# A linear-attention block with an MLP on one Trainium2 core: two transposes go from TensorE to DMA, and the order of the start and of the second layer norm changes

## The chip, the cores and the metric

The kernel runs on one core of a Trainium2 chip. The metric is the device time of one execution in microseconds (us), lower is better. The engines run side by side, each through its own list of instructions in order, and wait for each other by semaphores: PE (TensorE, matrix products), DVE (VectorE), ACT (ScalarE), POOL (GpSimd) and SP (SyncE). Here SP issues all DMA transfers.

## The reference, cut to what matters

Input x has 2048 rows of 512; there are 32 heads of 16; the MLP is 1792 wide. All is bf16.

```
def _layernorm(x, axis=-1, eps=1e-5):
    m = jnp.mean(x, axis=axis, keepdims=True)
    v = jnp.var(x, axis=axis, keepdims=True)
    return (x - m) / jnp.sqrt(v + eps)
phi = lambda t: jnp.where(t > 0, t + 1, jnp.exp(t)) + 1e-6
...
pq, pk = phi(q), phi(k)
kv = jnp.einsum("bhsd,bhse->bhde", pk, v)
z = jnp.einsum("bhsd->bhd", pk)
num = jnp.einsum("bhqd,bhde->bhqe", pq, kv)
den = jnp.einsum("bhqd,bhd->bhq", pq, z)[..., None] + 1e-6
o = num / den
...
h = x + _A_ref(_layernorm(x, axis=-1), A_wqkv, A_wo)
h2 = h + _B_ref(_layernorm(h, axis=-1), B_w1, B_w2)
```

_B_ref is max(y @ w1, 0) @ w2.

## The kernel before

The 2048 rows are 16 tiles of 128 (t), in 4 chunks of 512 (c, tiles 4c to 4c+3). The order of all work is written out by hand: the string ORDER is a list of words, each a small function with its numbers, and every engine gets its instructions in the order of the words. A word's name is the function op_ with that name. A number that names a PSUM bank (there are eight of 512 float32) is not needed below. The words that matter:

- Start, per tile: lx loads x (SP); S and A are the statistics (bn_stats, bn_aggr; DVE, L248, L249); R is 1/std (two ACT instructions, L254, L255); N normalises (DVE, L262); T transposes the tile by four PE transposes (L287) and E copies them from PSUM (ACT, L297); from tile 5 on X transposes by one DMA instead (SP, L308). The result lnT has the features on the partitions.
- K (per tile, 4 matmuls of 512 columns, L316) and Q (per chunk and block of 128 features, 4 matmuls, L324) are the projections of keys and queries. F, U, M, D and qF, qU, qM, qD make phi of them (two on ACT, two on DVE). lk and lq load their weights, wk_sb and wq_sb.
- G, z, kv, m: the sums over all rows, folded with wv and wo into m_sb.
- Per chunk: d4 the denominators (PE), dl4 and dx4 their reciprocals (ACT), wb stores these to DRAM (SP, L468), eight rb load them back, spread over the partitions (SP, L471), and dm multiplies the queries by them (two DVE instructions, L484, result pqs).
- Per tile, the second layer norm: h (4 matmuls from pqs, L493), hD adds x (DVE, L499), s and a the statistics (L250, L251), n subtracts the mean (DVE, L270; nA does the same on ACT, L276), and x transposes by DMA (L309), or t by PE with v copying on DVE (L306). r is 1/std (ACT), applied only at the end.
- Per chunk and block f of 128 of the MLP's 1792: p (4 matmuls of 512 columns, L508; ph does it in two halves of 256 columns, tiles 0, 1 and tiles 2, 3, L517), and pD (DVE, L528) or pA (ACT, L523) evicts two blocks with the relu. Then per tile f (14 matmuls, L537), fo (DVE, L545: times 1/std plus h) and fd (the store, SP, L552; four buffers).

PE, DVE and SP take their words strictly in turn, so a word that waits holds all later words of its engine. What keeps a word from its engine is its inputs, its PSUM bank, and its buffer. All rb of all chunks write one buffer, rr. A transposing DMA of one tile is one instruction on SP, an rb eighth is one too.

In the first chunk before the change, tiles 0 and 1 of the second layer norm are normalised on ACT (nA) and transposed by DMA, tiles 2 and 3 are normalised on DVE and transposed by PE. Only the blocks f = 0 to 3 are done in halves.

Of the kernel before, what the change touches and what calls it, by code (L numbers as in the profile page):

```python
# [15 lines left out]


ORDER = """
table const masks warm.70.7.64 warm.2.7 lx.0.1 S.0 A.0 R.0.1 lx.1.1 S.1 lx.2.1 A.1 N.0 T.0.1 lk.0.4 S.2 R.1.1
N.1 T.1.2 lx.3.1 A.2 E.0 K.0.4 R.2.1 lx.4.2 S.3 N.2 T.2.1 E.1 A.3 S.5 R.3.1 K.1.0.0.2 K.1.0.2.2 N.3 S.4 A.5 A.4  # L20
E.2 T.3.2 K.2.6.0.2 K.2.6.2.2 F.0.1 M.0.1 lx.6.2 E.3 S.7 lq.0.4 R.4.2 lx.8.4 Q.0.3.1 N.4 U.0.1 A.7 F.1.1 F.2.1
T.4.2 N.5 S.6 Q.0.1.4 U.1.1 M.1.1 A.6 lx.12.4 M.2.1 D.0.1 R.6.2 K.3.7.0.2 K.3.7.2.2 E.4 X.5 U.2.1 U.3.1 D.1.1
N.6 Q.0.0.3 N.7 S.10 qF.0.0.2 K.4.5 K.5.6 S.8 A.10 S.9 A.8 qU.0.0.2 S.12 F.4.2 D.2.1 X.6 Q.0.2.0 A.9 A.12 K.6.2
S.13 S.11 M.4.2 A.11 A.13 U.4.2 D.4.2 F.3.1 R.8.2 N.9 M.3.1 X.7 K.7.3 R.12.2 R.10.2 N.8 F.6.2 D.3.1 N.13 S.15
G.0 G.1 U.6.2 S.14 X.9 X.8 N.10 A.14 A.15 N.12 qM.0.0.2 M.6.2 X.13 qF.0.2.2 R.14.2 qU.0.2.2 qM.0.2.2 N.11 G.2
G.3 G.5 G.4 N.14 X.12 K.9.3 K.8.2 K.13.1 N.15 qD.0.0.2 D.6.2 za.4.1 X.11 X.10 F.8.2 U.8.2 M.8.2 K.12.0 U.12.2
F.12.2 G.7 za.6.0 K.11.3 D.8.2 qD.0.2.2 M.12.2 za.8.0 K.10.2 F.10.2 X.14 G.8 K.14.0 U.10.2 X.15 K.15.1 M.10.2 zf
lv.2.2 lv.0.2 G.9 D.10.2 zhi D.12.2 F.14.2 G.6 G.10 G.11 M.14.2 zlo U.14.2 D.14.2 z.0.0 z.2.0 z.3.0 z.1.0 G.14
lo.0.2 lo.2.2 zc zh d4.0.1 dl4.0 l1.0.2 G.13 G.12 G.15 dx4.0 gA.2.2 Q.1.1.3 Q.1.0.2 qF.1.0.2 gD.0.2 kv.1.4
kv.3.4 kv.0.4 kv.2.4 kx qU.1.0.2 qM.1.0.2 qD.1.0.2 Q.1.3.1 Q.1.2.0 qF.1.2.2 m.0.2 m.1.3 mD.0.2 m.3.7 m.2.6 wb.0  # L30
Q.2.0.4 Q.2.1.5 rb.0.7 rb.0.1 rb.0.6 rb.0.3 rb.0.0 rb.0.2 rb.0.4 rb.0.5 l1.2.2 qM.1.2.2 qU.1.2.2 Q.2.3.1
qD.1.2.2 mA.2.2 qF.2.0.2 Q.2.2.0 qU.2.0.2 dm.0.2.2 dm.0.0.2 qM.2.0.2 h.1.6 hD.1 s.1 a.1 qU.2.2.2 d4.1.3 dl4.1
h.0.7 hD.0 s.0 dx4.1 h.2.6 h.3.5 a.0 l2.0.7 wb.1 hD.2 nA.1 hD.3 qF.2.2.2 nA.0 s.2 s.3 Q.3.0.2 Q.3.1.3 a.2
Q.3.3.6 a.3 qF.3.0.2 qU.3.0.2 Q.3.2.5 x.1 r.0.4 qF.3.2.2 n.2 t.2.7 n.3 t.3.4 qD.2.0.2 v.2 v.3 x.0 ph.0.3.1.0
ph.0.1.3.0 ph.0.2.0.0 ph.0.3.1.1 qM.2.2.2 qM.3.0.2 ph.0.0.2.0 ph.0.0.2.1 qM.3.2.2 qD.3.0.2 qU.3.2.2 qD.2.2.2
ph.0.2.0.1 qD.3.2.2 p.0.7.5 d4.2.6.2 pD.0.2.2 dl4.2 dl4.3 rb.1.4 rb.1.6 rb.1.3 rb.1.2 rb.1.0 rb.1.1 ph.0.1.3.1
rb.1.7 rb.1.5 p.0.6.4 dx4.2 dm.1.0.2 dm.1.2.2 h.4.0 pD.0.0.2 hD.4 pD.0.6.2 p.0.5.1 h.6.6 dx4.3 p.0.4.0 hD.6
l2.7.7 h.5.4 pA.0.4.2 s.4 s.6 hD.5 h.7.7 a.4 a.6 p.0.11.6 p.0.10.5 s.5 hD.7 a.5 p.0.9.4 wb.2 rb.2.6 n.4 rb.2.0
rb.2.4 s.7 n.6 rb.2.3 rb.2.2 rb.2.1 a.7 n.5 n.7 rb.2.5 rb.2.7 dm.2.0.2 dm.2.2.2 pD.0.10.2 p.0.13.1 p.0.12.0
p.0.8.3 pD.0.12.2 wb.3 r.4.4 rb.3.0 rb.3.4 h.10.7 hD.10 x.6 h.8.2 h.11.6 hD.8 s.10 rb.3.5 rb.3.1 rb.3.6  # L40
f.1.0.0.7 rb.3.3 rb.3.2 rb.3.7 s.8 hD.11 pD.0.8.2 h.9.5 f.3.1.0.7 x.7 x.5 s.11 a.8 hD.9 f.1.0.7.7 f.0.4.0.7 a.10
a.11 x.4 dm.3.2.2 dm.3.0.2 h.14.7 h.12.3 s.9 n.11 h.15.6 a.9 n.10 h.13.2 fo.1 n.9 n.8 hD.14 s.14 hD.12 x.11
hD.15 f.0.4.7.7 r.8.4 p.1.13.7 p.1.6.3 a.14 hD.13 s.12 s.15 s.13 a.12 a.15 a.13 n.14 p.1.12.6 n.13 f.3.1.7.7
n.12 n.15 p.1.2.5 fo.0 pD.1.12.2 x.10 p.1.7.4 fo.3 p.1.3.6 x.9 pD.1.6.2 pD.1.2.2 r.12.4 x.8 p.1.11.2 p.1.10.1
pD.1.10.2 f.2.4.0.7 p.2.0.6 p.2.1.7 f.2.4.7.7 pD.2.0.2 p.2.10.0 p.2.11.1 fo.2 x.14 p.2.6.2 p.2.7.3 x.15 fd.3
p.2.13.7 p.2.12.6 pD.2.10.2 pD.2.6.2 x.12 fd.1 pD.2.12.2 p.2.2.0 x.13 fd.0 p.2.3.1 p.1.5.6 p.1.4.5 pD.2.2.2
pD.1.4.2 p.1.0.3 p.1.1.4 p.1.9.1 p.1.8.0 pD.1.0.2 pD.1.8.2 f.4.4.0.7 f.4.4.7.7 fo.4 fd.4 f.5.3.0.7 f.5.3.7.7
fo.5 fd.2 f.6.7.0.7 f.6.7.7.7 fo.6 p.2.4.2 p.2.5.3 f.7.0.0.7 f.7.0.7.7 pD.2.4.2 fo.7 p.3.6.1 p.3.7.2 pD.3.6.2
p.3.8.3 p.3.9.4 p.3.5.1 pD.3.8.2 p.3.4.0 pD.3.4.2 fd.6 p.3.10.3 p.3.11.4 pD.3.10.2 p.3.2.0 p.3.3.1 p.3.0.5
p.3.1.6 pD.3.2.2 pD.3.0.2 p.3.13.3 fd.7 p.3.12.2 pD.3.12.2 f.10.1.0.7 f.15.2.0.14.3.1 f.15.7.0.14.0.2 p.2.8.4  # L50
p.2.9.5 fo.15.3.1 fd.15.3.1 fo.15.0.2 pD.2.8.2 f.8.7.0.7 f.10.1.7.7 fo.10 f.8.7.7.7 fo.8 f.14.2.0.7 f.14.2.7.7
f.13.3.0.7 fd.5 fd.8 fd.10 fo.14 f.13.3.7.7 fo.13 f.9.0.0.7 f.9.0.7.7 fd.15.0.2 f.11.6.0.7 f.11.6.7.7 fd.13 fo.9
f.12.0.0.7 fd.9 f.12.0.7.7 fo.11 fd.14 fd.11 fo.12 fd.12 f.15.2.0.14.2.1 fo.15.2.1 fd.15.2.1
"""


# [1 line left out]
def kernel(  # L58
# [166 lines left out]
    def op_tw(n):
        rows = A_wqkv.rearrange("(r s) n -> r s n", s=A_wqkv.shape[0] // n)
        nc.scalar.dma_start(out=first_w[0:n, 0, :], in_=rows[:, 0, D : D + 4])

    def op_tx(n):
        rows = xf.rearrange("(r s) d -> r s d", s=S // n)  # L230
        nc.scalar.dma_start(out=first_x[0:n, :], in_=rows[:, 0, 0:4])

    def op_ta():
        nc.scalar.dma_start(out=first_w[:], in_=wqkv_v[:, :, D : D + 4])
# [234 lines left out]

    def op_rb(c, h):  # L470
        nc.sync.dma_start(  # L471
            out=rr[h * DH : (h + 1) * DH, :, :],
            in_=scr[c][:, h, :, :].rearrange("j o n -> o j n").broadcast_to([DH, KD, CW]),
        )
# [6 lines left out]

    def op_dm(c, jb, n):
        i = (c * KD + jb) % NQ
        nc.vector.tensor_tensor(  # L484
            out=pqs[:, i : i + n, :], in0=pqT[c][:, jb : jb + n, :], in1=rr[:, jb : jb + n, :], op=ALU.mult
        )


# [99 lines left out]
```

## Time and profile before

| | us |
|---|---|
| median of 3 runs | 169.63 (169.54 to 170.61) |
| the profiled execution, its own time | 169.66 |
| its span, first to last instruction | 168.0 |
| PE busy | 162.7 (97%) |
| DVE busy | 115.6 (69%) |
| ACT busy | 49.5 (29%) |
| granted TensorE clock | 1.00 |

The profile is one execution. "PE" is the matmuls, "PEld" the loads of their stationary operands, which overlap matmuls. A group's line gives the source line, the engine, result and input by the program's names, the count, the busy time and what ended the idle time before. In the chain of waits, each piece is the time in which the work that ended last moved on, by line. In the list of waits a line reads: who waited, for whom, total us, times, longest. In the timeline a row is the start, the length, the engine and line, and in brackets how long the engine was idle before, and for what. SPq is SP's queue of DMA issues; its times are those of issuing, and a transfer lands later.

### The profile page before, as it was taken

The numbers are of one execution on the slowest core, as the hardware profiler recorded it, in microseconds if no ns is written. First come the engines' busy times: TensorE is split into PE (matmuls) and PEld (weight loads), VectorE is DVE, ScalarE is ACT, GpSimd is POOL, SyncE is SP. The second block draws the span as 40 slices with busy tenths as digits, with TensorE's granted clock in tenths as the row PEclk, the third lists the DMA queues.
The fourth block names the chain that finished last, engine by engine and source line by source line (L and its number), as shares of the span: only waits on it lengthen the run. The fifth ranks groups of instructions, "written<-read, shape, count | busy, mean of one in ns | idle before, by whom it ended". The sixth has DMA issues, their size and how long they took to land.

```text
span 168.0 us, 2417 instructions
## 1 busy us (share of the span) xinstructions
PE 162.7 (97%) x924; PEld 79.2 (47%) x924; DVE 115.6 (69%) x217; ACT 49.5 (29%) x83; POOL 4.8 (3%) x21
## 2 busy tenths in 40 slices
...
GB/s 108 353 298 88 20 106 95 189 301 45 132 337 161 98 205 132 132 48 123 83 102 57 126 63 0 0 0 0 62 31 35 0 0 7 32 34 48 31 94 39
DMA packets 25003, 16.01 MB, mean 95 GB/s; under 512 B 15008, under 2 KB 23968, under 8 KB 24992
## 3 DMA queue, kind: packets, MB, share of 16 engines
...
q8 instruction: 7, 0.11, 0.3%
q14 instruction: 4, 0.03, 0.1%
HBM read 9.96 MB, written 2.62 MB: 75 GB/s over the span
## 4 chain that ended last, share of the span: by engine, by line
PE 92%; DMA 4%; SPq 2%; DVE 1%; issue 0%
PE bk L537 28%; PE bk L508 27%; PE bk L324 8%; PE bk L368 8%; PE bk L493 8%; PE bk L316 7%; DMA wq_sb<-in_A_wqkv_dram 4%; PE bk L517 2%; SPq L214 2%; PE bk L440 1%; DVE gT L545 1%; PE bk L392 1%; PE bk L414 1%; PE bk L426 1%; PE bk L287 0%
## 5 line engine op out<-in xcount | busy, mean ns | idle before, releaser
L537 PE MATMUL bk<-w_sb,at 128*128 128x512 bf16 (+2 forms) x252 | 50.0, 355 | 0.0
L508 PE MATMUL bk<-lnT,w_sb 128*128 128x512 bf16 x208 | 46.9, 379 | 0.0
L528 DVE TENSOR_SCALAR at<-bk 128x1024 bf16<-128x1024 f32 x27 | 32.8, 1223 | 13.2 <-PE bk L508 13.2
L537 PEld LDWEIGHTS <-at 128*128 128x128 bf16 x252 | 23.5, 98 | 25.4
L508 PEld LDWEIGHTS <-w_sb 128*128 128x128 bf16 x208 | 20.4, 98 | 23.9
L545 DVE SCALAR_TENSOR_TENSOR gT<-bk,rstd,h_nat 128x512 bf16<-128x512 f32 (+2 forms) x18 | 12.4, 691 | 24.6 <-PE bk L537 22.0
L334 ACT ACTIVATE eb<-bk 128x1024 bf16<-128x1024 f32 (+1 forms) x18 | 16.6, 929 | 5.3 <-PE bk L316 2.8
L337 ACT ACTIVATE rb<-bk 128x1024 bf16<-128x1024 f32 (+1 forms) x18 | 16.4, 929 | 0.0
L324 PE MATMUL bk<-lnT,wq_sb 128*128 128x512 bf16 x64 | 15.1, 379 | 0.3 <-DMA wq_sb<-in_A_wqkv_dram 0.3
L316 PE MATMUL bk<-wk_sb,lnT 128*128 128x512 bf16 x64 | 15.3, 379 | 0.0
L493 PE MATMUL bk<-m_sb,pqs 128*128 128x512 bf16 x64 | 15.1, 379 | 0.0
L368 PE MATMUL bk<-at,h_nat 128*128 128x512 bf16 x56 | 13.1, 379 | 0.0
L248 DVE BATCH_NORM_STATS2 st<-x_nat 128x6 f32<-128x512 bf16 x16 | 10.6, 678 | 2.3 <-DMA x_nat<-in_A_x_dram 2.3
L499 DVE TENSOR_TENSOR h_nat<-bk,x_nat 128x512 bf16<-128x512 f32 x16 | 10.6, 676 | 0.9 <-PE bk L493 0.9
L254 ACT ACTIVATE rstd<-mv,eps 128x2 f32<-128x2 f32 (+2 forms) x14 | 4.2, 297 | 23.7 <-DVE mv L251 20.9
L250 DVE BATCH_NORM_STATS2 st<-h_nat 128x6 f32<-128x512 bf16 x16 | 10.5, 684 | 0.1
L324 PEld LDWEIGHTS <-wq_sb 128*128 128x128 bf16 x64 | 6.1, 98 | 7.7 <-DMA wq_sb<-in_A_wqkv_dram 0.8
L493 PEld LDWEIGHTS <-pqs 128*128 128x128 bf16 x64 | 6.1, 98 | 7.7 <-DVE pqs L484 0.6
L368 PEld LDWEIGHTS <-h_nat 128*128 128x128 bf16 x64 | 6.1, 98 | 7.3 <-issue 0.2
L316 PEld LDWEIGHTS <-lnT 128*128 128x128 bf16 x64 | 6.1, 98 | 6.8
L341 DVE TENSOR_SCALAR eb<-eb 128x1024 bf16<-128x1024 bf16 (+1 forms) x18 | 6.6, 389 | 0.0
L262 DVE TENSOR_SCALAR h_nat<-x_nat,mv,rstd 128x512 bf16<-128x512 bf16 x16 | 6.3, 408 | 0.2 <-ACT rstd L255 0.2
...
## 6 DMA issues: line engine op xcount, KB each, us to landing
...
```

The lines of the kernel that those rows point to most:

```text
L248: op_S = lambda t: nc.vector.bn_stats(out=st[:, t, :], in_=x_nat[:, t, :])
L316: nc.tensor.matmul(bk[:, b, :], lhsT=lnT[c][:, kd, j * P : (j + 1) * P], rhs=wk_sb[:, kd, :], start=(kd == 0), stop=(kd == KD - 1),)
L324: nc.tensor.matmul(bk[:, b, :], lhsT=wq_sb[:, kd, j * P : (j + 1) * P], rhs=lnT[c][:, kd, :], start=(kd == 0), stop=(kd == KD - 1),)
L334: nc.scalar.activation(out=buf(eb, kind, i, n), in_=bank(at_bank[kind, i], n), func=ACT.Exp)
L337: nc.scalar.activation(out=buf(rb, kind, i, n), in_=bank(at_bank[kind, i], n), func=ACT.Relu)
L368: nc.tensor.matmul(bk[:, KD + kd, :], lhsT=ln_nat[:, t, kd * P : (kd + 1) * P], rhs=pk(t)[:, 0, :], start=(not stated), stop=(len(stated) ...
L493: nc.tensor.matmul(bk[:, b, :], lhsT=pqs[:, (c * KD + jb) % NQ, j * P : (j + 1) * P], rhs=m_sb[:, jb, :], start=(jb == 0), stop=(jb == KD ...
L499: nc.vector.tensor_tensor(out=h_nat[:, t : t + n, :], in0=bank(at_bank["h", t], n), in1=x_nat[:, t : t + n, :], op=ALU.add,)
L508: nc.tensor.matmul(bk[:, b, :], lhsT=w1_sb[:, kd, f * P : (f + 1) * P], rhs=lnT[c][:, kd, :], start=(kd == 0), stop=(kd == KD - 1),)
L528: nc.vector.tensor_scalar(out=acts[c % 2][:, f : f + n, :], in0=bank(at_bank["p", c, f], n), scalar1=-1.0, scalar2=0.0, op0=ALU.mult, op1= ...
L537: nc.tensor.matmul(bk[:, b, 0 : w * P], lhsT=acts[c % 2][:, f, j * P : (j + 1) * P], rhs=w2_sb[:, f, k * P : (k + w) * P], start=(f == 0), ...
L545: nc.vector.scalar_tensor_tensor(out=o_t[:, t % NO, cols], in0=bk[:, at_bank["f", t, k], 0 : w * P], scalar=rstd2[:, t : t + 1], in1=h_nat ...
```

## The change

- Start: A.2 stands ahead of N.1 on DVE, N.2 ahead of S.3. K.3 (two words of two matmuls each) and Q.0.0 stand ahead of Q.0.3. The order of SP's loads of x and of the first weights stays.
- First chunk's second layer norm: nA.0, nA.1 become n.0, n.1 (on DVE); t.2, t.3, v.2, v.3 become x.2, x.3. The order of tiles is 1, 0, 3, 2 throughout; h.1 stands ahead of Q.2.3.
- On SP, x.1 and x.0 stand ahead of the store wb.1, then x.3, x.2, and then the eight rb.1.
- MLP of the first chunk: the blocks f = 6, 7 are done in halves as well, all six first halves stand ahead of the second halves; pA.0.4 (ACT) becomes pD.0.4 (DVE).
- rr becomes two buffers, one for even and one for odd chunks.
- The remaining words are the same, with other places and other banks. Three functions that no word uses are removed, with two small tiles of theirs, so lines from 223 on have smaller numbers afterwards: 12 less from the layer norms on.

The diff, with the order cut to the two places (before, then after):

```diff
-table const masks warm.70.7.64 warm.2.7 lx.0.1 S.0 A.0 R.0.1 lx.1.1 S.1 lx.2.1 A.1 N.0 T.0.1 lk.0.4 S.2 R.1.1
-N.1 T.1.2 lx.3.1 A.2 E.0 K.0.4 R.2.1 lx.4.2 S.3 N.2 T.2.1 E.1 A.3 S.5 R.3.1 K.1.0.0.2 K.1.0.2.2 N.3 S.4 A.5 A.4
-E.2 T.3.2 K.2.6.0.2 K.2.6.2.2 F.0.1 M.0.1 lx.6.2 E.3 S.7 lq.0.4 R.4.2 lx.8.4 Q.0.3.1 N.4 U.0.1 A.7 F.1.1 F.2.1
+table const masks warm.70.7.64 warm.2.7 lx.0.1 S.0 A.0 R.0.1 lx.1.1 S.1 lx.2.1 A.1 N.0 T.0.1 lk.0.4 S.2 A.2
+R.1.1 N.1 T.1.2 E.0 R.2.1 lx.3.1 N.2 K.0.4 lx.4.2 S.3 T.2.1 E.1 A.3 S.5 R.3.1 K.1.0.0.2 K.1.0.2.2 N.3 S.4 A.5
+A.4 E.2 T.3.2 K.2.6.0.2 K.2.6.2.2 F.0.1 M.0.1 lx.6.2 E.3 S.7 lq.0.4 R.4.2 lx.8.4 K.3.7.0.2 K.3.7.2.2 Q.0.0.3
...
-qD.1.2.2 mA.2.2 qF.2.0.2 Q.2.2.0 qU.2.0.2 dm.0.2.2 dm.0.0.2 qM.2.0.2 h.1.6 hD.1 s.1 a.1 qU.2.2.2 d4.1.3 dl4.1
-h.0.7 hD.0 s.0 dx4.1 h.2.6 h.3.5 a.0 l2.0.7 wb.1 hD.2 nA.1 hD.3 qF.2.2.2 nA.0 s.2 s.3 Q.3.0.2 Q.3.1.3 a.2
-Q.3.3.6 a.3 qF.3.0.2 qU.3.0.2 Q.3.2.5 x.1 r.0.4 qF.3.2.2 n.2 t.2.7 n.3 t.3.4 qD.2.0.2 v.2 v.3 x.0 ph.0.3.1.0
-ph.0.1.3.0 ph.0.2.0.0 ph.0.3.1.1 qM.2.2.2 qM.3.0.2 ph.0.0.2.0 ph.0.0.2.1 qM.3.2.2 qD.3.0.2 qU.3.2.2 qD.2.2.2
-ph.0.2.0.1 qD.3.2.2 p.0.7.5 d4.2.6.2 pD.0.2.2 dl4.2 dl4.3 rb.1.4 rb.1.6 rb.1.3 rb.1.2 rb.1.0 rb.1.1 ph.0.1.3.1
-rb.1.7 rb.1.5 p.0.6.4 dx4.2 dm.1.0.2 dm.1.2.2 h.4.0 pD.0.0.2 hD.4 pD.0.6.2 p.0.5.1 h.6.6 dx4.3 p.0.4.0 hD.6
+Q.2.2.1 rb.0.1 qF.2.0.2 dm.0.0.2 dm.0.2.2 h.1.6 qD.1.2.2 h.0.3 hD.1 s.1 d4.1.4 hD.0 l1.2.2 a.1 dl4.1 n.1 s.0
+dx4.1 h.3.5 a.0 n.0 l2.0.7 x.1 x.0 wb.1 hD.3 Q.2.3.2 s.3 qF.2.2.2 qU.2.2.2 a.3 h.2.3 hD.2 n.3 s.2 Q.3.2.4
+Q.3.3.5 a.2 n.2 Q.3.1.7 Q.3.0.6 x.3 x.2 qF.3.2.2 ph.0.2.0.0 qM.2.2.2 qM.2.0.2 r.0.4 qD.2.2.2 qM.3.2.2 qD.2.0.2
+qU.3.2.2 qF.3.0.2 ph.0.1.3.0 ph.0.0.2.0 rb.1.1 ph.0.3.1.0 ph.0.6.4.0 ph.0.7.5.0 qM.3.0.2 qD.3.2.2 rb.1.5 rb.1.6
+ph.0.2.0.1 ph.0.3.1.1 ph.0.6.4.1 ph.0.7.5.1 qU.3.0.2 qD.3.0.2 pD.0.2.2 d4.2.6.2 pD.0.6.2 ph.0.1.3.1 rb.1.3
+rb.1.7 rb.1.2 ph.0.0.2.1 pD.0.0.2 rb.1.4 dl4.2 rb.1.0 p.0.11.1 dl4.3 dm.1.0.2 dm.1.2.2 l2.7.7 dx4.2 p.0.5.5
+p.0.4.4 h.5.2 wb.2 pD.0.4.2 hD.5 h.4.6 hD.4 h.7.5 s.5 h.6.2 hD.7 a.5 rb.2.4 rb.2.1 hD.6 f.0.3.0.7 s.7 s.4 s.6
...
-    rr = big.tile([P, KD, CW], BF16, name="rr")
+    rr = [big.tile([P, KD, CW], BF16, name=f"rr{i}") for i in range(2)]
...
-            out=rr[h * DH : (h + 1) * DH, :, :],
+            out=rr[c % 2][h * DH : (h + 1) * DH, :, :],
...
-            out=pqs[:, i : i + n, :], in0=pqT[c][:, jb : jb + n, :], in1=rr[:, jb : jb + n, :], op=ALU.mult
+            out=pqs[:, i : i + n, :], in0=pqT[c][:, jb : jb + n, :], in1=rr[c % 2][:, jb : jb + n, :], op=ALU.mult
```

More of the change, by code (lines that the diff above doesn't have):

```diff
@@ L18 @@
 ORDER = """
-table const masks warm.70.7.64 warm.2.7 lx.0.1 S.0 A.0 R.0.1 lx.1.1 S.1 lx.2.1 A.1 N.0 T.0.1 lk.0.4 S.2 R.1.1
-N.1 T.1.2 lx.3.1 A.2 E.0 K.0.4 R.2.1 lx.4.2 S.3 N.2 T.2.1 E.1 A.3 S.5 R.3.1 K.1.0.0.2 K.1.0.2.2 N.3 S.4 A.5 A.4
-E.2 T.3.2 K.2.6.0.2 K.2.6.2.2 F.0.1 M.0.1 lx.6.2 E.3 S.7 lq.0.4 R.4.2 lx.8.4 Q.0.3.1 N.4 U.0.1 A.7 F.1.1 F.2.1
-T.4.2 N.5 S.6 Q.0.1.4 U.1.1 M.1.1 A.6 lx.12.4 M.2.1 D.0.1 R.6.2 K.3.7.0.2 K.3.7.2.2 E.4 X.5 U.2.1 U.3.1 D.1.1
-N.6 Q.0.0.3 N.7 S.10 qF.0.0.2 K.4.5 K.5.6 S.8 A.10 S.9 A.8 qU.0.0.2 S.12 F.4.2 D.2.1 X.6 Q.0.2.0 A.9 A.12 K.6.2
@@ L24 @@
[L24 to L28, printed above, removed]
@@ L29 @@
-lo.0.2 lo.2.2 zc zh d4.0.1 dl4.0 l1.0.2 G.13 G.12 G.15 dx4.0 gA.2.2 Q.1.1.3 Q.1.0.2 qF.1.0.2 gD.0.2 kv.1.4
-kv.3.4 kv.0.4 kv.2.4 kx qU.1.0.2 qM.1.0.2 qD.1.0.2 Q.1.3.1 Q.1.2.0 qF.1.2.2 m.0.2 m.1.3 mD.0.2 m.3.7 m.2.6 wb.0
-Q.2.0.4 Q.2.1.5 rb.0.7 rb.0.1 rb.0.6 rb.0.3 rb.0.0 rb.0.2 rb.0.4 rb.0.5 l1.2.2 qM.1.2.2 qU.1.2.2 Q.2.3.1
-qD.1.2.2 mA.2.2 qF.2.0.2 Q.2.2.0 qU.2.0.2 dm.0.2.2 dm.0.0.2 qM.2.0.2 h.1.6 hD.1 s.1 a.1 qU.2.2.2 d4.1.3 dl4.1
-h.0.7 hD.0 s.0 dx4.1 h.2.6 h.3.5 a.0 l2.0.7 wb.1 hD.2 nA.1 hD.3 qF.2.2.2 nA.0 s.2 s.3 Q.3.0.2 Q.3.1.3 a.2
@@ L34 @@
-Q.3.3.6 a.3 qF.3.0.2 qU.3.0.2 Q.3.2.5 x.1 r.0.4 qF.3.2.2 n.2 t.2.7 n.3 t.3.4 qD.2.0.2 v.2 v.3 x.0 ph.0.3.1.0
-ph.0.1.3.0 ph.0.2.0.0 ph.0.3.1.1 qM.2.2.2 qM.3.0.2 ph.0.0.2.0 ph.0.0.2.1 qM.3.2.2 qD.3.0.2 qU.3.2.2 qD.2.2.2
-ph.0.2.0.1 qD.3.2.2 p.0.7.5 d4.2.6.2 pD.0.2.2 dl4.2 dl4.3 rb.1.4 rb.1.6 rb.1.3 rb.1.2 rb.1.0 rb.1.1 ph.0.1.3.1
-rb.1.7 rb.1.5 p.0.6.4 dx4.2 dm.1.0.2 dm.1.2.2 h.4.0 pD.0.0.2 hD.4 pD.0.6.2 p.0.5.1 h.6.6 dx4.3 p.0.4.0 hD.6
-l2.7.7 h.5.4 pA.0.4.2 s.4 s.6 hD.5 h.7.7 a.4 a.6 p.0.11.6 p.0.10.5 s.5 hD.7 a.5 p.0.9.4 wb.2 rb.2.6 n.4 rb.2.0
@@ L39 @@
[L39 to L53, printed above, removed]
+table const masks warm.70.7.64 warm.2.7 lx.0.1 S.0 A.0 R.0.1 lx.1.1 S.1 lx.2.1 A.1 N.0 T.0.1 lk.0.4 S.2 A.2
```

38 lines of the change are left out of this document (27 added, 11 removed).

## The prediction

> **What bounds the kernel now.** I read the page's busy times first, then the stretches, the start of the timeline, the chain around the removed work, and last what SP's queue does there. Columns of the stretches: start:end, length, then busy us (and instructions) of PE, PEld, DVE, ACT, POOL, granted clock, DMA share, GB/s.
>
> ```profile
> PE 162.7 (97%) x924; PEld 79.2 (47%) x924; DVE 115.6 (69%) x217; ACT 49.5 (29%) x83; POOL 4.8 (3%) x21
> ```
> ```profile
> 5.00:10.40 5.40, 4.13 (x30) 1.85 (x30) 4.87 (x15) 4.43 (x14) 1.05 (x4) 1.00 1.07 380
> 10.40:35.80 25.40, 25.40 (x126) 11.72 (x127) 24.47 (x60) 20.74 (x34) 0.00 (x0) 1.00 0.51 126
> ...
> 60.00:75.00 15.00, 15.00 (x79) 6.71 (x78) 14.80 (x27) 3.83 (x7) 0.00 (x0) 1.00 0.42 129
> 75.00:101.00 26.00, 26.00 (x122) 11.77 (x121) 22.64 (x44) 1.00 (x4) 0.00 (x0) 1.00 0.42 92
> ```
>
> PE has no idle time from 10.4 us to its last matmul near 164.2; it idles only before 10.4. So the time changes in three ways only: less matmul work, less idle time before 10.4, or new holes after it. DVE is nearly full twice (24.47 of 25.40, 14.80 of 15.00), so it is where a hole would come from. The clock is 1.00 in every row, so all PE rows below hold in every stretch.
>
> ```profile
> 5.55 0.47 DVE L262 TENSOR_SCALAR h_nat<-x_nat,mv,rstd 128x512 bf16<-128x512 bf16 x1
> 5.95 0.16 DVE L249 BATCH_NORM_AGGREGATE mv<-st 128x2 f32<-128x6 f32 x1
> 6.08 0.23 PEld L287 LDWEIGHTS <-h_nat 128*128 128x128 bf16 x4 [0.77 <-DVE h_nat L262]
> ...
> 6.62 0.69 DVE L248 BATCH_NORM_STATS2 st<-x_nat 128x6 f32<-128x512 bf16 x1 [0.51 <-DMA x_nat<-in_A_x_dram]
> 7.23 0.40 DVE L262 TENSOR_SCALAR h_nat<-x_nat,mv,rstd 128x512 bf16<-128x512 bf16 x1
> ...
> 9.22 0.60 ACT L297 ACTIVATE lnT<-bk 128x512 bf16<-128x512 bf16 x1
> ...
> 10.38 1.04 PE L324 MATMUL bk<-lnT,wq_sb 128*128 128x512 bf16 x4 [0.33 <-DMA wq_sb<-in_A_wqkv_dram]
> ```
> DVE's order at the start is N.1, A.2, S.3, N.2; S.3 waited for tile 3 until 6.62 and N.2 stood behind it. At the end of the start-up PE waits for wq_sb (landed at 10.33) while K.3's input (E.3, 9.22 to 9.82) lies ready.
>
> ```profile
> 53.25 3.45 PE bk L324 x16
> 56.70 0.45 PE bk L287 x8
> 57.15 3.06 PE bk L517 x28
> ```
> ```profile
> 54.20 1.20 SPq L309 DMA_TRANSPOSE lnT<-hn  x1
> 55.58 3.73 SPq L471 DMA_DIRECT2D rr<-scr  x8
> ```
> ```profile
> PEld L493 <- DVE pqs L484: 0.6, 2, 0.3
> ```
> The chain holds t.2 and t.3 (eight PE transposes, 0.45 us). On SP the eight loads rb.1 follow the transposes x.1, x.0. The weight loads of h wait for DVE's multiply dm.1 by these loads; PE itself doesn't lose by it yet, since weights are loaded ahead.
>
> **The change, part by part.** PE's spacing comes from the chain: a 512-wide matmul 216 ns (0.86 us for 4), 256-wide 109 ns (3.06 for 28), a transpose 56 ns (0.45 for 8).
>
> 1. Start. A.2 now stands ahead of N.1, and N.2 ahead of S.3. S.2 ends at 5.64 (4.95 and 0.69), A.2 runs at 5.68, N.1 at 5.78 in place of 5.55, T.1 at 6.25 in place of 6.08. ACT is in E.0 until about 6.02, then runs R.2 (0.29, 0.20) to 6.55; N.2 starts at 6.59 in place of 7.23. S.3 follows 0.32 behind N.2's start, at 6.91 in place of 6.62; A.3 at 7.64 (7.54 before), and R.3, N.3, T.3, E.3 all about 0.09 later: E.3 ends at 9.9, K.2 runs 9.11 to 9.97. K.3 now comes ahead of the first Q: 4 x 216 ns, 9.97 to 10.83. The first Q then starts at 10.83 with wq_sb half a microsecond in place. Before it started at 10.38 with K.3 (0.86) still to do. Gain 10.38 + 0.86 - 10.83 = 0.41. SP's loads keep their order, so wq_sb's landing stays. Bounds: 0.50 (the whole hole from K.2's last issue to Q), and 0.0, if the pieces ahead slip by another 0.4; nearer the former, as every step has its row. With PE 0.41 earlier, K.7 comes at 17.1 and X.7's transpose (issued at 14.44, landed 2.45 later) is in at 16.9: cover 0.1 to 0.2.
>
> 2. t.2, t.3 go: 8 x 56 ns = -0.45. The halves of f = 6, 7: 16 x 109 in place of 8 x 216 ns, +0.02. Sum -0.43; PE has no hole there to swallow it, so the bounds are those of the sum.
>
> 3. x.3, x.2 by DMA. hD, s, a, n of tiles 1, 0, 3, 2 now follow each other on DVE; h.1 starts 1.28 earlier than before (0.41 from the start, 0.86 since Q.2.3 goes behind it), at 47.9. From hD.1's start to the fourth n took 5.91 before (50.26 to 56.17) with two n's; two more at 0.25 each and the later h.2 (behind Q.2.3) make it 6.9: n.2 starts at 55.9, ends at 56.2. x.3, behind the store wb.1, is issued at about 55.05; transposes follow each other at 1.30 on SP (14.03 us for 9 issues with some waits; the close ones 82.87, 84.16, 85.46), so x.2 goes out at 56.36 and lands 2.43 later, 58.79, usable at 58.85. PE begins the first halves at 56.54 - 0.41 = 56.13; six of them are 24 x 109 ns = 2.62, until 58.75. Hole +0.10. Bounds: 0, if x.2 is 0.1 earlier; 0.7, with the slowest row of hn's transposes (landing 3.0).
>
> 4. rb.1 behind them. First load at 57.66 (before 55.58), eight at 0.47, the last issued at 60.95; before, these landed in 2.8 to 3.0: 63.87. dm.1 starts 0.1 behind (61.80 to 61.92 before), at 63.98, and its halves are out at 64.66 and 65.27. PE: 58.85 + 2.62 (second halves) + 0.55 (d4.2, d4.3) + 3 x 0.864 (f = 11, 5, 4) = 64.61 at h.5, whose third matmul needs the second half: 64.61 + 0.43 = 65.04 against 65.31. Hole +0.27. Bounds: 0 and 0.5, the loads landing in 2.65 (their row in the next chunk) or some 0.2 late. The two holes aren't independent: if x.2 comes earlier, PE is earlier at h.5 and hole 4 takes what hole 3 leaves, so together they are 0.37 or hole 3, whichever is more. wb.1 hides: it lands 1.8 after its issue (about 54.1), under x.3 and x.2, and rb.1 stands behind those anyway.
>
> 5. DVE and ACT. DVE gets n.0, n.1 (2 x 0.34) and one eviction (1.22, pA to pD), loses two copies (2 x 0.42): +1.06 us in a stretch that is 14.80 of 15.00 full. What hides it: hD, s and a of tiles 4 to 7 have more than 10 us until their f's, and 75 to 101 has 3.4 us free. I take 0; if the cover is gone, up to +1.06. Two rr buffers take away the wait of rb.2 for dm.1; that was not on PE's path: 0.
>
> 6. The rest of the order. From h.8 on the same instructions stand in another order, with other banks: p, f, fo and fd of all chunks, and SP's last x among the stores. The last piece of PE (14 matmuls of 128 columns of tile 15), its fo and its store are as before, so the tail stays. The last x had landed by 98, its p begin near 127; out_dram's stores have 4 buffers, and the one wait of DVE for them (2.5 us) didn't reach PE. Cost 0; without that cover, a hole of some 0.25 per late eviction.
>
> Sum: -0.41 - 0.43 + 0.10 + 0.27 + 0 = -0.47. The profiled execution took 169.66 (span 168.0, 1.66 around it), so 169.19; the median is 0.03 lower, 169.63: 169.2 us.
>
> **The rivals.**
> A. No holes: x.2 and dm.1 come in time. Then -0.84: 168.8. For it: the holes are sums of many steps and no larger than a few of their errors; against: both come out late.
> B. A DMA transpose is worse here than PE's: it comes late and holds SP. The first transpose of h_nat (11.10) took 1.83 to issue and 3.4 to land, while loads of x were under way. If x.3 and x.2 go like that, x.2 is issued at 56.98 and lands at 60.4: a hole of 1.7, which covers hole 4; -0.84 + 1.7 = +0.86, 170.5. With one landing of 3.0 alone it is 0.7, and the time 169.5. Against: the other transposes lie at 2.4 to 2.5 but for that 3.0, and at 55 to 58 only wb.1 moves beside these. It decides, slower than before, from x.2 landing at 59.5 (a hole of 0.84). The Trainium skill, "VectorE: DVE Perf Modes", section Rules for kernel authors, speaks against the change in this way: for a 128x128 transpose take TensorE if a PSUM destination will do, the DMA crossbar otherwise. The trace has both prices, 0.22 us of PE for a tile's four blocks and 2.4 us to landing, and the forecast rests on the latter being hidden.
> C. Slower through DVE: its extra 1.06 us reaches PE in full, as evictions behind h.5 hold its banks, on top of the holes: -0.84 + 0.37 + 1.06 = +0.59, 170.2. It decides when evictions come 0.5 later than PE wants their banks; against: at 60 to 75 PE waited for none, though DVE was as full.
> D. The start gains nothing (N.1's delay of 0.23 and a late X.7 pass through): -0.43 + 0.37 = -0.06, 169.6.
>
> **How the numbers follow.** Forecast (the sum, within 0.25) 0.55, A 0.12, D 0.12, B 0.10, C 0.07; 0.04 remains for what I don't see. Predicted 169.2. A sets the low, 168.7; the high 170.1 takes in D and B's milder half and leaves out C and the rest of B. No case but an unseen one is over 1% from 169.63 (below 167.9, above 171.3), about what a measurement of this kernel can tell from no change: faster 0.03, same 0.92, slower 0.05.
>
> **What would show it.** Step 1: first Q near 10.83, not waiting for wq_sb. Step 2: L287's hn group gone, 48 256-wide matmuls. Step 3: a PE hole of 0.1 near 58.8 ended by a transpose. Step 4: one of 0.3 near 65 ended by pqs. Step 5: no PE hole ended by DVE's evictions from 65 to 101. A PE hole of over 0.8 after 10.8, or a first Q after 11.2, makes the prediction wrong.

## The result: 0.5% slower, and the profile after

| | before | after |
|---|---|---|
| median of 20 runs, us | 169.62 (169.16 to 170.61) | 170.64 (169.64 to 171.75) |
| ratio after / before | | 1.0053, 95% interval 1.0037 to 1.0069 |
| the profiled execution, us | 169.66 | 170.72 |
| its span, us | 168.0 | 169.0 |

I forecast 169.2 in a range of 168.7 to 170.1. The kernel is 1.0 us slower, above the range and on the other side of before. Lines in the changed kernel are 12 less from the layer norms on; in the experiments they shift by a few again.

First the busy times of the page and the two late stretches of the changed kernel (columns as before):

```profile
PE 162.0 (96%) x908; PEld 79.7 (47%) x924; DVE 117.1 (69%) x218; ACT 47.4 (28%) x80; POOL 4.8 (3%) x21
```
```profile
60.00:75.00 15.00, 14.38 (x79) 6.94 (x79) 13.11 (x22) 2.80 (x6) 0.00 (x0) 1.00 0.47 144
75.00:101.00 26.00, 25.51 (x116) 11.46 (x119) 24.64 (x49) 1.01 (x4) 0.00 (x0) 1.00 0.34 78
```

Both late stretches, full of PE before, now have idle PE: 0.62 and 0.49 us. DVE, full before at 60 to 75, is idle 1.89 us there although it has more to do. So PE and DVE both wait for something else. The chain of waits names it (start, length, what), first around h.8 in the kernel before, then in the changed one:

```profile
73.38 2.59 PE bk L493 x12
```

```profile
56.52 2.62 PE bk L505 x24
...
59.17 1.92 PE bk L505 x16
...
63.28 4.41 DMA scr<-rd
...
71.18 1.71 DMA rr<-scr
72.89 1.55 issue
...
74.63 0.70 DVE pqs L472
...
75.38 2.94 PE bk L481 x12
```

Between 50 and 80 us, the chain of before was PE alone. Now it leaves PE at 61.45, goes through wb.2, the store of the third chunk's reciprocals (4.41 us, 1.86 before: 63.27 to 65.12), its eight loads rb.2 and the multiply dm.2, and returns to PE at 75.38 with h.8. PE's timeline shows the hole:

```profile
70.01 4.48 PE L496 MATMUL bk<-lnT,w_sb 128*128 128x512 bf16 x19
75.38 1.43 PE L481 MATMUL bk<-m_sb,pqs 128*128 128x512 bf16 x5 [0.90 <-DVE pqs L472]
```

The block products p before h.8 began at 70.01, and 20 of 216 ns (one of them has no row in the trace) are done at 74.33: a hole of 1.05 us, and one of 0.17 for dm.2's second half. Before, dm.2 ran at 71.47 with no wait.

Why does the store take 4.41 us? SP's timeline of before, then of after:

```profile
55.58 3.73 SPq L471 DMA_DIRECT2D rr<-scr  x8
59.35 0.43 SPq L220 DMA_DIRECT2D w_sb<-in_B_w_dram  x1
63.27 0.34 SPq L468 DMA_DIRECT2D scr<-rd  x1
65.17 3.89 SPq L471 DMA_DIRECT2D rr<-scr  x8
```
```profile
57.99 3.81 SPq L459 DMA_DIRECT2D rr<-scr  x8
61.85 0.43 SPq L219 DMA_DIRECT2D w_sb<-in_B_w_dram  x1
63.28 0.34 SPq L456 DMA_DIRECT2D scr<-rd  x1
67.71 4.61 SPq L459 DMA_DIRECT2D rr<-scr  x8
```

The word behind rb.1 on SP is l2.7.7: one load of the second half of w2 (7 blocks of 128 KB, 896 KB; first used after 78 us). With rb.1 it went from 59.35 to 61.85. By the trace's landing events it lands at 64.81 before and at 67.36 after, 5.5 us behind its issue both times. The store wb.2, issued at 63.27 and 63.28, lands 0.3 us behind the load both times: 65.12 and 67.69, 2.57 later. But before it is issued 1.5 us before the load lands, and takes the 1.7 to 1.9 us of a store alone; after it is issued 4.1 us before.

By this alone dm.2 would be ready for h.8 at 74.66 (rb.2's last landing 71.07 + 2.57, 0.27 to dm.2 and 0.75 to h.8 as in the chain), a hole of 0.33. The other 0.72 is rb.2 itself: its last load, issued at 71.18, takes 3.2 us to land (74.36), in before 2.3. The difference lies in its issue on SP, which takes 1.14 us, the longest of the 32; before, the longest took 0.53 (the loads rb of both kernels by their line: shortest, median and longest issue in ns). From the end of the issue to the landing it is 2.0 us both times.

```profile
L471 SPq DMA_DIRECT2D rr<-scr x32: 303/424/529, 41.2 to 77.8; - x32
L459 SPq DMA_DIRECT2D rr<-scr x32: 303/424/1138, 41.0 to 79.3; - x32
```

The list of DMA queues from 69 to 75 us (packets, MB, share of 16 engines) shows what moves beside it:

```profile
q8 instruction: 1, 0.02, 1.0%
q14 instruction: 1, 0.01, 0.5%
```

The packet of queue 8, 16 KB for the instructions, starts at 71.03 and takes 0.93 us; that of queue 14, 8 KB, starts at 70.98 and takes 0.50. In before the former moves at the same 71.03, when rb.2 is in and wb.3 is under way: that store took 4.0 us, and fifteen of the sixteen completions that the trace has for each transfer were in after 2.1. The three loads ahead of the last one in after are the same: fifteen completions come within 2.5 us, and the sixteenth makes one of them 3.6. Long issues on SP go with this packet too: in eight of the thirteen profiled executions, the changed kernel's and those of the runs below among them, SP issues two loads rb around the packet's start, and the second issue takes 0.65 to 1.18 us. So the lateness seems to push rb.2 under this packet; no run took the packet away, so this part is an observation.

The account, with before's and after's rows:

| | forecast | measured | from |
|---|---|---|---|
| start | -0.41 | -0.18 | first Q at 11.06 with K.3 (0.86) done; before at 10.38 with K.3 to do |
| t.2, t.3 removed, more halves | -0.43 | -0.43 | eight transposes gone, 48 halves, counted at the spacing of the rows |
| x.2 by DMA | +0.10 | +0.20 | landed 59.13; halves go on at 59.17 |
| dm.1 at h.5 | +0.27 | 0 | dm.1 at 63.99, h.5 at 65.04, PE not waiting |
| DVE, ACT, rr | 0 | 0 | no wait of PE for an eviction from 65 to 101 |
| dm.2 at h.8 | none | +1.22 | 1.05 and 0.17, above |
| sum | -0.47 | +0.81 | the last two fo begin at 165.06 against 164.22: +0.84 |

The rows for the start, then for dm.1 and h.5, in the changed kernel's timeline:

```profile
11.06 1.03 PE L312 MATMUL bk<-lnT,wq_sb 128*128 128x512 bf16 x4
```
```profile
63.99 1.29 DVE L472 TENSOR_TENSOR pqs<-pqT,rr 128x1024 bf16<-128x1024 bf16 x2
65.04 3.62 PE L481 MATMUL bk<-m_sb,pqs 128*128 128x512 bf16 x16
```

### The profile page after: what moved, and what is told of

It is laid out like the page before. It is cut to its first block, busy times and chain, and to the rows that moved or that the text cites. A ratio compares the mean times of both kernels' runs of the same rounds, so it can differ in the third digit from the quotient of the medians.

```text
span 169.0 us, 2400 instructions
## 1 busy us (share of the span) xinstructions
PE 162.0 (96%) x908; PEld 79.7 (47%) x924; DVE 117.1 (69%) x218; ACT 47.4 (28%) x80; POOL 4.8 (3%) x21
## 4 chain that ended last, share of the span: by engine, by line
PE 86%; DMA 4%; DVE 2%; issue 2%; ACT 2%; SPq 2%; DVEq 0%
PE bk L525 27%; PE bk L496 21%; PE bk L356 8%; PE bk L312 8%; PE bk L304 7%; PE bk L481 6%; PE bk L505 3%; DMA scr<-rd 3%; PE bk L233 3%; SPq L459 2%; DMA rr<-scr 1%; ACT ld L434 1%; DVE st L236 1%; DVE gT L533 1%; PE bk L275 1%
## 5 line engine op out<-in xcount | busy, mean ns | idle before, releaser
L525 PE MATMUL bk<-w_sb,at 128*128 128x512 bf16 (+2 forms) x247 | 49.5, 355 | 0.3
L496 PE MATMUL bk<-lnT,w_sb 128*128 128x512 bf16 x195 | 43.7, 379 | 0.3
L516 DVE TENSOR_SCALAR at<-bk 128x1024 bf16<-128x1024 f32 x28 | 34.0, 1222 | 12.9 <-PE bk L496 9.9
L496 PEld LDWEIGHTS <-w_sb 128*128 128x128 bf16 x200 | 19.6, 98 | 23.4
```

Of the source, the lines that this page charges most:

```text
L496: nc.tensor.matmul(bk[:, b, :], lhsT=w1_sb[:, kd, f * P : (f + 1) * P], rhs=lnT[c][:, kd, :], start=(kd == 0), stop=(kd == KD - 1),)
L516: nc.vector.tensor_scalar(out=acts[c % 2][:, f : f + n, :], in0=bank(at_bank["p", c, f], n), scalar1=-1.0, scalar2=0.0, op0=ALU.mult, op1= ...
L525: nc.tensor.matmul(bk[:, b, 0 : w * P], lhsT=acts[c % 2][:, f, j * P : (j + 1) * P], rhs=w2_sb[:, f, k * P : (k + w) * P], start=(f == 0), ...
```

## The experiments

The theories: W, the load: wherever the 896 KB of l2.7.7 move, a store or load issued meanwhile lands only when they have landed; the change moved them 2.5 us later, into wb.2. Rivals: U, the store or rb.2 is slow by itself (other order, two rr buffers). V, DVE's new order makes dm.2 late. For the start: S, the new order makes it hang on how early PE gets to full speed, since S.3 stands behind N.2 and so behind T.0 on PE.

**The load behind rb.2.** In the changed kernel, one word moved:

```diff
-... dm.1.0.2 dm.1.2.2 l2.7.7 dx4.2 ... rb.2.5 rb.2.3 pD.0.10.2 ...
+... dm.1.0.2 dm.1.2.2 dx4.2 ... rb.2.5 rb.2.3 l2.7.7 pD.0.10.2 ...
```

> The changed kernel, with only one word moved: the load of w2's second half (l2.7.7, 896 KB) stands behind the eight rb.2 in place of behind rb.1. Theory W (that load is under way when the store wb.2 is issued and holds it: 4.4 us to landing in place of 1.9, then rb.2, dm.2 and h.8 are late): wb.2 lands in about 1.9, the last rb.2 near 71.3 in place of 74.4, no PE hole of 0.95 near 75; 1.0 to 1.1 less than the changed kernel, 169.5. Rival V (DVE, with 1.06 us more to do, is what holds dm.2): dm.2 as late as before, 170.5. Rival U (a store to DRAM is slow by itself here now and then; before the change wb.3 took 4.0 with no load of weights under way): wb.2 still near 4, 170.5.

Measured 171.65 us, ratio to before 1.0102 (1.0061 to 1.0143): slower still, where W had 169.5. SP's timeline, then PE in the chain of waits:

```profile
65.24 3.88 SPq L457 DMA_DIRECT2D rr<-scr  x8
69.18 0.52 SPq L217 DMA_DIRECT2D w_sb<-in_B_w_dram  x1
69.81 0.49 SPq L454 DMA_DIRECT2D scr<-rd  x1
76.25 0.78 SPq L457 DMA_DIRECT2D rr<-scr  x2
```
```profile
84.37 2.07 PE bk L479 x8
```

The hole at 75 is gone: wb.2 lands in 1.7 us, and h.8 follows its p without a break. But the load now lands at 76.04, and wb.3, issued 0.6 behind it, at 76.20, 6.4 us after its issue (fifteen of its sixteen completions are in after 5.2; the packet of queue 8 moves at 73.87). rb.3 and dm.3 come late, and PE has a hole of 1.85 us before 84.37. I missed the time, since I had not asked what is issued next; the hole moved with the load, which is W and not U or V.

**The load from ACT's queue.** Is it SP's order or the transfer itself? The load issued by ACT behind dl4.3 (al2 is l2 with the scalar engine's DMA):

```diff
-... p.0.11.1 dl4.3 dm.1.0.2 dm.1.2.2 l2.7.7 dx4.2 ...
+... p.0.11.1 dl4.3 al2.7.7 dm.1.0.2 dm.1.2.2 dx4.2 ...
```

> The changed kernel, with l2.7.7 issued by ACT behind dl4.3, so at about the same time (62.3) but from another engine's queue. ACT's dx4.2 and so wb.2 come some 0.4 later. Theory W in the form that wb.2 stands behind the load in SP's own queue: wb.2 lands in about 2, the hole near 75 shrinks by 1 to 0.3 or less, 169.7 to 170.0. Theory W in the form that the load takes the DMA engines themselves: wb.2 lands when the load does, near 67.8, and the hole stays: 170.6 to 171. Rivals V and U: 170.5 to 171.

Measured 170.65 us, 1.0052 (1.0027 to 1.0077), as the changed kernel. ACT's row, then SP's:

```profile
62.22 0.41 ACTq L223 DMA_DIRECT2D w_sb<-in_B_w_dram  x1
```
```profile
63.81 0.34 SPq L457 DMA_DIRECT2D scr<-rd  x1
```

The load lands at 67.7 and the store, from another queue, 0.3 behind it: 4.2 us. The packets of the two can be told apart here: the load's 896 of 1 KB move from 63.31 to 67.25, the store's 128 only from 66.51 to 67.59, the first 2.7 us after its issue; with no load under way, in the run before this one, it is 0.85. So the two meet behind the queues, not in SP's list. The Trainium skill, "DMA: Bandwidth & Descriptors", section Issuing engines are not separate DMA queues, says that transfers run on the same 16 engines whichever engine starts them; these packets agree. The hole at h.8 is 0.5 us here, as PE comes there 0.5 later by its start (first Q at 11.59).

**The kernel before, with its load made late.** Five loads of 16 KB into a spare tile, ahead of l2.7.7 (they do work that the reference doesn't ask for):

```diff
-... p.0.4.0 hD.6 l2.7.7 h.5.4 ...
+... p.0.4.0 hD.6 du.0 du.1 du.2 du.3 du.4 l2.7.7 h.5.4 ...
```

> The kernel before, with five further loads (16 KB of w1 each, into a tile that nothing reads) on SP ahead of l2.7.7, so that this is issued about 2.3 later (61.7 in place of 59.35), as in the changed kernel, and nothing else is changed. Theory W: wb.2 (issued at 63.3) lands near 67.3 in place of 65.1, rb.2's last near 73.3, and PE gets a hole at h.8 to h.11; 0.3 to 1.3 slower than before, 169.9 to 170.9. Rivals V and U: wb.2 in 1.9, 169.6.

Measured 172.48 us, 1.0149 (1.0099 to 1.0199), above the 169.9 to 170.9 of theory W; the profiled execution took 171.76. SP's rows, and PE's at h.8:

```profile
61.75 0.42 SPq L220 DMA_DIRECT2D w_sb<-in_B_w_dram  x1
63.34 0.35 SPq L468 DMA_DIRECT2D scr<-rd  x1
67.16 4.83 SPq L471 DMA_DIRECT2D rr<-scr  x8
```
```profile
68.12 5.34 PE L514 MATMUL bk<-lnT,w_sb 128*128 128x512 bf16 x24
75.00 1.21 PE L499 MATMUL bk<-m_sb,pqs 128*128 128x512 bf16 x4 [1.54 <-DVE pqs L490]
```

Nothing of the change is in this kernel but the load's lateness (61.75; the changed kernel 61.85), and the hole is there: 24 products of 216 ns from 68.12 end at 73.30, h.8 starts at 75.00, 1.7 us later. The five spare loads are in by 62.97, before the store is issued. This speaks against V, and against U as far as it lies in the order or the two buffers: DVE's order and rr are those of before. The hole is longer than in the changed kernel as PE comes to h.8 earlier; why the median of the six runs lies 0.7 above the profiled one, the profile doesn't show.

**The load ahead of rb.1.**

```diff
-... x.3 x.2 qF.3.2.2 ... dm.1.2.2 l2.7.7 dx4.2 ...
+... x.3 x.2 l2.7.7 qF.3.2.2 ... dm.1.2.2 dx4.2 ...
```

> The changed kernel, with l2.7.7 ahead of the eight rb.1 (right behind x.2), so issued near 58 and landed near 63.5, before wb.2. Theory W: wb.2 in 1.9, no hole near 75; but now the eight rb.1 stand behind the load: the last lands 64.5 to 66 in place of 63.9, dm.1 and h.5 late, a hole of 0.5 to 2 near 65. Time between 169.9 and 171.5. Rivals V and U: both holes, over 171.

Measured 172.25 us, 1.0127 (1.0079 to 1.0175), above the 169.9 to 171.5 of theory W, in which the profiled execution lies (171.25). The chain, then PE at h.5:

```profile
58.30 5.38 DMA rr<-scr
```
```profile
62.13 2.75 PE L494 MATMUL bk<-lnT,w_sb 128*128 128x512 bf16 x12
66.63 3.58 PE L479 MATMUL bk<-m_sb,pqs 128*128 128x512 bf16 x15 [1.74 <-DVE pqs L470]
```

Now the loads rb.1 pay: the first takes 5.38 us in place of 2.7, dm.1 comes late, and PE has a hole of 1.9 before h.5 (12 x 216 ns from 62.13 end at 64.72). At 75 there is none. Of the places tried, the changed kernel's own is not the worst.

**The load right behind the first half of w2**, near 46 us, with the changed start and with that of before (the words up to E.2; K.3 ahead of Q in both):

```diff
-... n.0 l2.0.7 x.1 x.0 wb.1 ...
+... n.0 l2.0.7 l2.7.7 x.1 x.0 wb.1 ...
```

> The changed kernel, with l2.7.7 right behind l2.0.7, so issued near 45.6 while SP otherwise stands still until 51.8; the two loads ahead of it moved 896 KB in about 2.5 us each, so it should land near 54.6. Theory W (the load of w2's second half costs whatever store or load is issued while it moves, on whichever queue): x.1 is held by some 0.6, wb.1 (54.4) and wb.2 (63.3) land in 1.9, the last rb.2 near 71.3, no hole over 0.2 after 60; time as forecast for the change but for the start, 169.2 to 169.6. Rival V2 (without that load the change is still slower, by the transposes, DVE and the new order): 170.2 or more.

> As the kernel with l2.7.7 right behind l2.0.7, with the order of before the change from the beginning to E.2 (N.1 ahead of A.2, S.3 ahead of N.2); K.3 stays ahead of the first Q. Theory S (in the new order S.3 stands behind N.2, and so behind R.2, E.0 and T.0, so that a clock of PE that is granted late, or a late T.0, reaches K.3 in full; in the old one S.3 waits for its tile alone): 0.1 to 0.5 faster than with the new start, 168.9 to 169.3. Rival (the order of the start is worth its forecast 0.1): 0.1 slower than with the new start.

Measured 170.47 us, 1.0037 (1.0017 to 1.0058), and with the old start 169.98, 1.0015 (0.9994 to 1.0036). Both lie above the ranges of theories W and S, and the first in that of V2. The rows of the first, the chain and PE:

```profile
53.66 3.79 DMA lnT<-hn
```
```profile
57.59 2.67 PE L503 MATMUL bk<-lnT,w_sb 128*128 128x256 bf16 x23 [0.54 <-DMA lnT<-hn]
```

The load lands at 56.5. Now the transposes x.1 and x.0 are held, 4.6 and 3.8 us in place of 2.4, and the first halves of the MLP have a hole of 0.7; I had expected 0.6 for x.1. So transposes are held as well as stores and plain loads. There is no hole behind this one, and wb.2 lands in 1.7 us. Most of the rest of what lies over before is the start (first Q at 11.59), so its time doesn't speak for V2.

**The start by itself.** In the kernel before: K.3 ahead of the first Q, and nothing else; then the changed kernel's order of the start on top:

```diff
-... lx.8.4 Q.0.3.1 N.4 ... R.6.2 K.3.7.0.2 K.3.7.2.2 E.4 ...
+... lx.8.4 K.3.7.0.2 K.3.7.2.2 Q.0.3.1 N.4 ... R.6.2 E.4 ...
```
```diff
-... S.2 R.1.1 N.1 T.1.2 lx.3.1 A.2 E.0 K.0.4 R.2.1 lx.4.2 S.3 N.2 T.2.1 ...
+... S.2 A.2 R.1.1 N.1 T.1.2 E.0 R.2.1 lx.3.1 N.2 K.0.4 lx.4.2 S.3 T.2.1 ...
```

> The kernel before, with nothing but K.3's two words moved ahead of the first Q. If the hole before the first Q (0.49 in the profile) is a wait for wq_sb that K.3 can fill: 0.3 to 0.5 faster, 169.1 to 169.3. If it is refilled by a late E.3, or what follows then waits for DVE: 169.5 to 169.7.

> The kernel before, with K.3 ahead of the first Q and the changed kernel's order from the beginning to E.2 (A.2 ahead of N.1, N.2 ahead of S.3). My prediction's step 1 put this at -0.41: 169.2. Theory S: the same as before the change or 0.1 to 0.3 faster on the median, with more spread, and slower than with K.3 alone moved: 169.3 to 169.6.

Measured 169.44 us, 1.0000 (0.9977 to 1.0023), and 169.74, 1.0006 (0.9982 to 1.0029), beside 169.61 for before. Neither can be told from no change: K.3 alone falls between its two cases, and the new start lies above its 169.3 to 169.6. Both spans are 167.5, 0.5 below before's, so in the one profiled execution the start did gain what I forecast, with and without the new order of DVE. Its twelve runs with the new order fall into two groups, five from 169.16 to 169.29 and seven from 169.66 to 170.01.

**The load where little else moves.** SP is idle from 16 to 19 us, between the transposes X.7 and X.9. In the changed kernel, then with the old start:

```diff
-... S.15 X.7 R.8.2 N.9 ... dm.1.2.2 l2.7.7 dx4.2 ...
+... S.15 X.7 l2.7.7 R.8.2 N.9 ... dm.1.2.2 dx4.2 ...
```

> The changed kernel with one word moved: the second half of w2 (l2.7.7) is loaded right behind the transpose X.7, near 16 us, where SP is idle until X.9 at about 19.4 and few other transfers move. Theory W (the 896 KB load holds whatever is issued while it moves, and that is the whole late loss): no hole of PE near 75, 66 or 57; wb.2 under 2.5 us; only the hole of about 0.2 for x.2 remains, so the time is the changed kernel's less 1.1: 169.4 to 169.8, by how late the clock starts (its own start order is kept). Rival: the loss at 75 has another cause too (DVE's order), then a hole of over 0.3 stays near 75 and the time is above 170. Risk: X.9 waits for the load, K.9 comes late, a hole near 22.

> As the run before, and with the order of the kernel before up to the third tile's copies (E.2), K.3 ahead of the first Q. Theories W and S (the new order of the start hangs on the clock's start) together: start hole about 2.4, x.2's hole 0.2, no others: PE's work 161.5 and 2.9 of holes, 169.0 to 169.3, 0.3 to 0.6 below the kernel before, and 0.2 to 0.5 below the run before. Against S: the two runs are the same within 0.1.

Measured 169.99 us, 1.0009 (0.9991 to 1.0027), and 169.49, 0.9996 (0.9979 to 1.0013), beside 169.58. The first lies above the 169.4 to 169.8 of theory W and just under the rival's 170; its profiled execution took 169.34, so the profile is of one of its faster runs. Its rows of SP and PE:

```profile
15.84 0.57 SPq L217 DMA_DIRECT2D w_sb<-in_B_w_dram  x1
```
```profile
63.16 0.34 SPq L454 DMA_DIRECT2D scr<-rd  x1
```
```profile
69.88 4.48 PE L494 MATMUL bk<-lnT,w_sb 128*128 128x512 bf16 x19
74.20 2.10 PE L479 MATMUL bk<-m_sb,pqs 128*128 128x512 bf16 x9
```

wb.2 lands in 1.7 us, and 20 products (19 have rows) from 69.88 end at 74.20, where h.8 starts: no hole there, nor at 57, 66 or 84. One hole is left after the start, 0.26 us, for x.2. The load lands at 21.75 and stretches X.9 to 3.1 us, for which PE doesn't wait. The instruction packet comes at 71.10, behind rb.2. With one word moved, no late hole but x.2's is left and the time can't be told from before's, so W accounts for the late loss: the load's lateness, and what that pushes rb.2 into. The time of the run with the old start, 169.49, lies above the 169.0 to 169.3 written down for it.

The two kernels differ in the start alone, and their medians by 0.50 us, as those with the load behind l2.0.7 did (0.49). The intervals of their ratios overlap both times, so it is for the rows to tell. Where it comes from is seen best in two profiled executions with the same slow beginning. First PE, then DVE in the kernel with the load behind l2.0.7 and the changed start; then PE and DVE in the kernel with the load behind X.7 and the old start:

```profile
5.61 0.92 PE L273 MATMUL bk<-ident,h_nat 128*128 128x128 bf16 x8 [0.22 <-DVE st L234]
...
9.63 0.40 PE L273 MATMUL bk<-ident,h_nat 128*128 128x128 bf16 x4 [0.57 <-DVE h_nat L248]
```
```profile
7.33 0.41 DVE L248 TENSOR_SCALAR h_nat<-x_nat,mv,rstd 128x512 bf16<-128x512 bf16 x1 [1.28 <-ACT rstd L241]
7.66 0.69 DVE L234 BATCH_NORM_STATS2 st<-x_nat 128x6 f32<-128x512 bf16 x1
```
```profile
5.61 0.91 PE L273 MATMUL bk<-ident,h_nat 128*128 128x128 bf16 x8 [0.22 <-DVE st L234]
...
8.90 0.40 PE L273 MATMUL bk<-ident,h_nat 128*128 128x128 bf16 x4
```
```profile
6.58 0.69 DVE L234 BATCH_NORM_STATS2 st<-x_nat 128x6 f32<-128x512 bf16 x1 [0.52 <-DMA x_nat<-in_A_x_dram]
7.33 0.41 DVE L248 TENSOR_SCALAR h_nat<-x_nat,mv,rstd 128x512 bf16<-128x512 bf16 x1
```

Both executions transpose tile 0 at 107 ns a block (its four start at 5.61, 5.72, 5.82 and 5.93) in place of 56, and N.2 runs at 7.33 in both, behind ACT's copies of the tiles before. With the old order S.3 is done in the meantime, at 6.58, and T.3 runs at 8.90; with the new one DVE sits idle for 1.28 us, S.3 starts at 7.66, and T.3 at 9.63, 0.73 later. All thirteen profiled executions fit. With the old order T.3 starts between 8.79 and 9.24, whether T.0 starts at 5.00 or at 5.61. With the new one it goes with T.0: 8.79 to 8.92 where T.0 starts at 5.0, 9.10 at 5.33 (the changed kernel), 9.28 at 5.51, 9.63 at 5.61. So where PE is at full speed by 5 us the new order does no harm, as in the changed kernel with the load behind X.7, whose runs go from 169.22 to 170.13, while all but one with the old start lie between 169.2 and 169.71. The granted clock of these stretches reads 1.00, so the slow beginning shows only in PE's spacing. The Trainium skill, "TensorE: Matmul & The Clock Gate", Part 1, says that the array runs at half rate until a window of about 3.4 us has been busy, and that the window runs freely, so that the moment differs from run to run; the two spacings, 107 and 56 ns, agree with this.

**The load among the first weights.** With the old start, behind the first half of w1 near 32 us:

```diff
-... lo.2.2 l1.0.2 kv.2.6 ... dm.1.2.2 l2.7.7 dx4.2 ...
+... lo.2.2 l1.0.2 l2.7.7 kv.2.6 ... dm.1.2.2 dx4.2 ...
```

> As the run before, but the second half of w2 goes out right behind the first half of w1, near 32.5 us, with four other weight loads under way. W: it lands near 42, the store wb.0 (issued at 39.2) lands with it in place of at 41.0, rb.0 and dm.0 come some 1 us later. If dm.0 has that much to spare, 169.0 to 169.3 as in the run before; if not, a hole of up to 1 us near 47 and up to 170.2.

Measured 170.74 us, 1.0067 (1.0045 to 1.0089), above both ranges. The chain:

```profile
39.11 3.14 DMA scr<-rd
...
49.13 1.22 PE bk L479 x4
```

The load lands at 41.9, the store wb.0 with it, 3.14 us after its issue in place of 1.7, and dm.0 holds h.1: a hole of 1.1 us at 49.1. The same mechanism, in the first chunk.

## Why the prediction was wrong

1. The start: right in kind, mis-sized, 0.41 forecast and 0.18 measured. wq_sb was no longer waited for, as I said. I costed N.2 and S.3 by one execution of before, in which PE was fast early, and so fixed the moment when T.0 and E.0 free ACT; and I took a granted clock of 1.00 to mean that PE's rows hold in every stretch, which the 107 and 56 ns at the start contradict. The moment isn't fixed: in the changed kernel's profile T.0 starts at 5.33, in that of before at 5.09, and this 0.24 is about what the gain lacks. N.2 came at 6.80, not 6.59, T.3 at 9.10, and in another execution at 9.63. The bound "0.0, if the pieces ahead slip by another 0.4" was there, and rival D with it, but not the reason.
2. t.2 and t.3: right, -0.43.
3. x.2: right in kind, 0.20 for 0.10. Its issue was 0.32 later than forecast (56.68), of which the start's lateness is 0.23, and it took 2.45 as its rows said. Rival B didn't come in its form, a late x.2. But its other half, that a transpose holds SP, did: x.3 and x.2 take SP from 55.39 to 57.89, and by this 2.5 us the load behind rb.1 went later. So the rule cited there from the Trainium skill ("VectorE: DVE Perf Modes", Rules for kernel authors), TensorE for a 128x128 transpose, isn't refuted here: DMA transposes cost PE 0.20 at x.2 and saved it 0.43, but what they pushed back on SP's queue cost it 1.22.
4. **The failed step.** Step 4 moves rb.1 from 55.58 to about 58 and follows it to dm.1 and h.5. That dm.1 came within 0.01 us of the forecast (63.99) is luck: the loads were issued 0.3 to 0.4 later than I said and landed in 2.5 us in place of 2.9. The step then stops: "wb.1 hides" was the only queue neighbour it looked at. Of what stands behind the moved words on SP, it left out l2.7.7 and wb.2, and so put the wait of dm.2 and h.8 at nothing: the load went 2.5 us later, the store was issued 4.1 us before the load landed in place of 1.5, and it took 4.41 us in place of 1.86. With rb.2 slowed behind it, PE got the holes of 1.05 and 0.17 at h.8. A hole of over 0.8 is what the prediction itself named as a sign against it. That this could cost something was to be seen beforehand: wb takes 1.7 to 4.0 us in the kernel before (the 4.0 by one late completion of sixteen, so from another cause, and the measured 4.41 is more), and the slack was to be read off, rb.2's landing at 71.07, 0.27 to dm.2 and 0.75 to h.8 at 73.38, 1.3 us. The two holes in the sum were as I said not independent: PE came later to h.5 and the second was nothing.
5. DVE and ACT: right, the cover held. "Two rr buffers take away the wait of rb.2 for dm.1": worth nothing, as I said: rb.2 waited for wb.2 in both kernels (landed 65.12, issued 65.17; 67.69 and 67.71).
6. The rest of the order: right as far as PE shows it; none of the four rivals named a transfer that isn't moved by name but only stands behind those that are.

What stays open: whether it is the instruction packet that holds the issue of rb.2's last load (0.72 of the 1.05). Where rb.2 is in before the packet, as with the load behind X.7, its loads take 2.3 to 2.6 us; where not, as in the changed kernel, up to 3.6. Taking it away wasn't tried. That x.3 and x.2 are what moves the load is read from SP's rows; no run had the rest of the change with t.2 and t.3 in their place. Also open is whether the change without its two faults gains anything: 169.49 against 169.58, with an interval of -0.2 to +0.1%. In the two profiled executions the last fo begin 0.54 earlier (163.68 against 164.22), about what PE's work (-0.43), the start (first Q at 10.86 with K.3 done, -0.38) and x.2 (+0.23) make together, but that is one execution of each.
